# Opening of a fused attention and feed-forward kernel: constants moved between engines, statistics in tiles of their own, later queries in another PSUM bank

## The chip, the cores and the metric

The kernel runs on one core of one Trainium2 chip. The metric is the device time of one execution in microseconds (us), given as the median of several runs. PE is TensorE's matrix multiply, PEld its weight load, DVE is VectorE, ACT is ScalarE and POOL is GpSimd.

## The reference

One transformer block on 2048 rows of 512 features: layer norm, attention with 32 heads of 16, a residual, layer norm, a gated feed-forward part with 1792 hidden features, a residual. Inputs are bfloat16. The code is shortened.

```python
def _A_ref(x, wqkv, wo):                      # H = 32, Dh = 16
    qkv = (x @ wqkv).reshape(B, S, 3, H, Dh).transpose(2, 0, 3, 1, 4)
    q, k, v = qkv[0], qkv[1], qkv[2]
    scores = jnp.einsum("bhqd,bhkd->bhqk", q, k) * (Dh ** -0.5)
    o = jnp.einsum("bhqk,bhkd->bhqd", softmax(scores), v)
    return o.transpose(0, 2, 1, 3).reshape(B, S, D) @ wo
# ... _B_ref: (sigmoid(x @ w_gate) * (x @ w_up)) @ w_down
h  = x + _A_ref(_layernorm(x), wqkv, wo)
h2 = h + _B_ref(_layernorm(h), w_gate, w_up, w_down)
```

What matters here is how the kernel gets the softmax's sum: a constant column next to V makes that sum a column of the product with V. V stands in a tile `Vaug` of 16 blocks of rows by 32 heads by 17 columns, whose 17th column is a constant, 0.5.

## The kernel before

A static planner in Python orders the opening. It ends with the first scores, and the first exp (an ACTIVATE into `pt`) is the start of the steady state, in which PE and ACT are both almost always busy. The parts that the change touches are these. First the constants:

```python
Vaug = const.tile([P, NT, H, VW], BF16)          # P=128, NT=16, H=32, VW=17, DH=16
QT = [const.tile([P, QC], BF16, name=f"QT{g}") for g in range(NG)]
QTB = const.tile([P, 2, QC], BF16, name="QTb")
# ...
nc.vector.memset(eps_t[:], 1e-5)
nc.scalar.activation(out=A0[:], in_=eps_t[:], func=ACT.Sqrt)     # "warm": loads the Sqrt table
fill = prep.tile([P, QC], BF16, name="fill")
nc.gpsimd.memset(fill[:], 1.0)
nc.gpsimd.memset(eps4_t[:], 4e-5)
nc.gpsimd.memset(power[:], -0.5)
ramp = prep.tile([P, 2, 32], BF16, name="ramp")
for k in range(32):
    nc.gpsimd.memset(ramp[:, 0, k:k + 1], float(k))
nc.gpsimd.tensor_scalar(out=eps4_t[:], in0=eps4_t[:], scalar1=1.0, scalar2=None, op0=ALU.mult)
# ...
nc.vector.memset(Vaug[:, :, :, DH:VW], 0.5)      # 512 elements of 2 bytes, 34 bytes apart
nc.vector.memset(QTB[:], 0.0)
nc.vector.memset(ident_bf[:], 0.0)
nc.vector.transpose(out=ramp[:, 1, :], in_=ramp[:, 0, :])        # then the identity and the masks
```

Then the order of the opening. Each word is an engine's letter and a task: `s` statistics of a row tile, `q` Sqrt, `r` reciprocal, `a` apply, `t` transpose, `e` copy out of PSUM, `p0`/`p1` projection to keys/queries, `kt`/`qt` copies of keys and queries, `exps` the load of the exp table, `zero` the zeroing of a bank.

```python
START = "As1 Ds0 Ds2 Aq0 Dr0 Da0 Pt0 Aq2 Df1 Ds3 Aq1 Azero Ae0 Pp10 Dr2 Da2 Aq3 Aexps Dr1 Da1 Dr3 Da3 Pt2 De2 Pt1 Pp00 Pt3 Ae3 Pp12 De1 Pp01 Dkt0 Pp11 Dqt0 Pp13 Aqt1".split()
BANKS = {("t", 0): 5, ("t", 2): 7, ("t", 1): 6, ("t", 3): 1, 0: 2, 1: 3}

mvs = [small.tile([P, TQ, nc.vector.BN_AGGR_DIM], FP32, name="mv") for c in range(NQC)]
rstds = [small.tile([P, TQ], FP32, name="rstd") for c in range(NQC)]
def root(i):
    A.activation(out=rstds[0][:, i:i + 1], in_=mvs[0][:, i, 1:2], func=ACT.Sqrt, bias=eps_t[:, 0:1])
def proj0(which, i):
    ps = buf[which] if which in buf else buf.setdefault(which, bank0(which))
    for d in range(DC):
        E.matmul(ps[:, i * P:(i + 1) * P], lhsT=w0[:, which, d, :], rhs=xnv[0][:, i, d, :],
                 start=(d == 0), stop=(d == DC - 1))
def query0(half, a, act=False):
    cs = slice(0, QC) if half is None else slice(half * 2 * P, (half + 1) * 2 * P)
    # ... ACT or DVE: QT[a][:, cs] = buf[1][:, cs] * maskz[:, a]
# ... after the opening's words, the second query tile as a whole on DVE:
query0(None, 1)
```

Of the kernel before, what the change touches and what calls it, by code (L numbers as in the profile page):

```python
# [8 lines left out]
FP32 = mybir.dt.float32  # L9
# [5 lines left out]
ALU = mybir.AluOpType  # L15
ACT = mybir.ActivationFunctionType
# [5 lines left out]

START = "As1 Ds0 Ds2 Aq0 Dr0 Da0 Pt0 Aq2 Df1 Ds3 Aq1 Azero Ae0 Pp10 Dr2 Da2 Aq3 Aexps Dr1 Da1 Dr3 Da3 Pt2 De2 Pt1 Pp00 Pt3 Ae3 Pp12 De1 Pp01 Dkt0 Pp11 Dqt0 Pp13 Aqt1".split()

# [122 lines left out]
def kernel(  # L147
# [11 lines left out]
    nc = tc.nc  # L159
    P = 128  # L160
    S, D = A_x.shape[1], A_x.shape[2]
    H, DH = 32, 16
    F = B_w_gate.shape[1]
    NT = S // P
# [4 lines left out]
    QC = 512  # L169
    NQC = S // QC  # L170
    TQ = QC // P
# [12 lines left out]
    VW = DH + 1  # L184
# [21 lines left out]
    eps_t = const.tile([P, 1], FP32)  # L206
    eps4_t = const.tile([P, 1], FP32)
    mask = const.tile([P, 2], FP32)
    maskz = const.tile([P, 2], FP32)
# [3 lines left out]
    KT = [const.tile([P, S], BF16, name=f"KT{p}") for p in range(NP)]  # L213
    QT = [const.tile([P, QC], BF16, name=f"QT{g}") for g in range(NG)]
    QTB = const.tile([P, 2, QC], BF16, name="QTb")
    QTb = [QTB[:, a, :] for a in range(2)]
    Vaug = const.tile([P, NT, H, VW], BF16)
# [8 lines left out]
    xb = [prep.tile([P, TQ, D], BF16, name=f"xb{c}") for c in range(NQC)]  # L226
# [24 lines left out]
    nc.scalar.activation(out=A0[:], in_=eps_t[:], func=ACT.Sqrt)  # L251
    fill = prep.tile([P, QC], BF16, name="fill")
    nc.gpsimd.memset(fill[:], 1.0)
    nc.gpsimd.memset(eps4_t[:], 4e-5)
# [7 lines left out]
    acc = PS[:, 0, :]  # L262
    nc.vector.memset(Vaug[:, :, :, DH:VW], 0.5)
    nc.vector.memset(QTB[:], 0.0)
    nc.vector.memset(ident_bf[:], 0.0)
# [5 lines left out]
    def masks():  # L271
        nc.vector.tensor_reduce(out=mask[:], in_=ident_bf[:].rearrange("p (b a d) -> p a b d", a=2, d=DH),
                                axis=AX.XY, op=ALU.max)
        nc.vector.tensor_scalar(out=maskz[:], in0=mask[:], scalar1=ZS, scalar2=None, op0=ALU.mult)

    masks()

    def stats1(src, st):
# [55 lines left out]

    BANKS = {("t", 0): 5, ("t", 2): 7, ("t", 1): 6, ("t", 3): 1, 0: 2, 1: 3}

    def bank0(key):
        return PS[:, BANKS[key], :]

    mvs = [small.tile([P, TQ, nc.vector.BN_AGGR_DIM], FP32, name="mv") for c in range(NQC)]  # L340
    rstds = [small.tile([P, TQ], FP32, name="rstd") for c in range(NQC)]
    buf = {}
# [12 lines left out]
    V, A, E = nc.vector, nc.scalar, nc.tensor  # L355

    def stats_task(c, i):
        src, mv = xb[c][:, i, :], mvs[c][:, i, :]

        def on_act():  # L360
            junk = work.tile([P, D], BF16, name="junk")
            A.activation(out=junk[:], in_=src, func=ACT.Identity, scale=1.0 / D,
                         accum_out=mv[:, 0:1])
            A.activation(out=junk[:], in_=src, func=ACT.Square, scale=D ** -0.5,
                         accum_out=mv[:, 1:2])
            buf["fix", c, i] = True
        if c == 0:
            Task("s%d" % i, ["x%d" % i], A=(1480, on_act), D=(850, lambda: ln_stats(src, mv)))
            Task("f%d" % i, ["s%d" % i], D=(290, lambda: fix(c, i)))

    def fix(c, i):
        mv = mvs[c][:, i, :]
        if ("fix", c, i) in buf:
            t = small.tile([P, 1], FP32, name="fix")
            V.tensor_tensor(out=t[:], in0=mv[:, 0:1], in1=mv[:, 0:1], op=ALU.mult)
            V.tensor_tensor(out=mv[:, 1:2], in0=mv[:, 1:2], in1=t[:], op=ALU.subtract)

    def root(i):
        A.activation(out=rstds[0][:, i:i + 1], in_=mvs[0][:, i, 1:2], func=ACT.Sqrt, bias=eps_t[:, 0:1])

    def apply(c, i):
        xn = buf["xn", c, i] = prep.tile([P, D], BF16, name="xn0", bufs=4)
        V.tensor_scalar(out=xn[:], in0=xb[c][:, i, :], scalar1=mvs[c][:, i, 0:1],
                        scalar2=rstds[c][:, i:i + 1], op0=ALU.subtract, op1=ALU.mult)

# [6 lines left out]
    def proj0(which, i):  # L392
        ps = buf[which] if which in buf else buf.setdefault(which, bank0(which))
        for d in range(DC):
            E.matmul(ps[:, i * P:(i + 1) * P], lhsT=w0[:, which, d, :], rhs=xnv[0][:, i, d, :],
                     start=(d == 0), stop=(d == DC - 1))

    def keys0(half, act):
        cs = slice(half * 2 * P, (half + 1) * 2 * P)
        (A.copy if act else V.tensor_copy)(out=KT[0][:, cs], in_=buf[0][:, cs])  # L400

    def query0(half, a, act=False):
        cs = slice(0, QC) if half is None else slice(half * 2 * P, (half + 1) * 2 * P)
        if act:
            A.activation(out=QT[a][:, cs], in_=buf[1][:, cs], func=ACT.Identity, scale=maskz[:, a:a + 1])
        else:
            V.tensor_scalar(out=QT[a][:, cs], in0=buf[1][:, cs], scalar1=maskz[:, a:a + 1], scalar2=None,
                            op0=ALU.mult)
    fixed("w0", 6800.0)
    for i in range(TQ):  # L410
        fixed("x%d" % i, (3700.0, 3500.0, 4250.0, 4000.0)[i])
        stats_task(0, i)
        fixed_by = "f%d" if "As%d" % i in START else "s%d"
        Task("q%d" % i, [fixed_by % i], A=(310, lambda i=i: root(i)))
        Task("r%d" % i, ["q%d" % i], D=(110, lambda i=i: V.reciprocal(
            out=rstds[0][:, i:i + 1], in_=rstds[0][:, i:i + 1])))
        Task("a%d" % i, ["r%d" % i], D=(345, lambda i=i: apply(0, i)))
        Task("t%d" % i, ["a%d" % i], P=(300, lambda i=i: turn0(0, i)))
        Task("e%d" % i, ["t%d" % i], A=(550, lambda i=i: copy0(0, i, A.copy)),
             D=(430, lambda i=i: copy0(0, i, V.tensor_copy)))  # L420
        for w in (1, 0):
            Task("p%d%d" % (w, i), ["e%d" % i, "w0"], P=(280, lambda w=w, i=i: proj0(w, i)))
    for h in range(2):
        Task("qt%d" % h, ["p1%d" % (2 * h), "p1%d" % (2 * h + 1)],
             A=(460, lambda h=h: query0(h, 0, True)), D=(480, lambda h=h: query0(h, 0)))
# [3 lines left out]
        out=small.tile([P, 1], FP32, name="warm")[:], in_=eps_t[:], func=ACT.Exp)))  # L429
# [18 lines left out]
    for word in START:  # L448
        t, eng = tasks[word[1:]], word[0]
# [9 lines left out]
    keep_warm(go)  # L459

    for q in [QTB[:, 1, :]] + [q[:] for q in QT[2:]]:
        nc.sync.dma_start(out=q, in_=QTB[:, 0, :])
# [7 lines left out]
    LAT = 60.0  # L470
    TAIL = {"A": 150.0, "D": 85.0, "G": 100.0}
    T = {e: max(0.0, free[e] - go) for e in free}
# [135 lines left out]
    DRAIN = 170.0  # L608
# [636 lines left out]
    half = []  # L1245
# [153 lines left out]
    pe_time("dense", 560.0)  # L1399
    query0(None, 1)  # L1400
    T["D"] = max(T["D"] + 660.0, T["P"] + DRAIN + LAT) + 430.0
    keys0(1, False)
# [132 lines left out]
    for i in range(QB):  # L1535
        t = dvx.tile([P, 3, GQ, QC], I16, name="J", bufs=QB)[:].rearrange("p a b n -> p (a b n)")
# [24 lines left out]
    mv = small.tile([P, n, nc.vector.BN_AGGR_DIM], FP32, name="mvl")  # L1561
# [114 lines left out]
```

## Time and profile before

| | before |
|---|---|
| median (range), 3 runs | 732.33 us (732.21 to 732.76) |
| span of the profiled execution | 730.9 us |
| busy shares PE, ACT, DVE, POOL | 96, 96, 91, 58% |
| start of the first exp | 13.13 us |
| end of the opening on DVE (two copies) | 10.38 us |

The rows of a timeline are: start in us, length in us, engine, line of the kernel, operation, destination and source with their shapes, count, and in brackets how long the engine had stood idle and what ended it. The prediction shows the rows of DVE, and of ACT from 7.59 us on. The rows of ACT that stand ahead of them in the same timeline of the kernel before:

```profile
3.59 0.63 ACT L362 ACTIVATE junk<-xb 128x512 bf16<-128x512 bf16 x1 [0.45 <-DMA xb<-in_A_x_dram]
...
5.84 0.29 ACT L379 ACTIVATE rstd<-mv,eps_t 128x1 f32<-128x1 f32 x1 [0.77 <-DVE mv L282]
```

ACT makes the statistics of tile 1 as soon as its load has landed, and is then done so early that the first Sqrt stands 0.77 us for DVE's statistics of tile 0. ACT has slack here and DVE has none. That slack is what the change spends.

### The profile page before, as it was taken

What the parts mean: (1) busy time and instruction counts of PE and PEld (TensorE: products, weight loads), DVE (VectorE), ACT (ScalarE), POOL (GpSimd) and SP (SyncE); (2) the same over time, 40 slices, a digit from 0 to 9 for tenths busy, and PEclk for the clock granted to TensorE, in tenths of its full rate; (3) what the DMA queues carried; (4) which work ended last, traced back from release to release, by engine and by line L of the source; (5) the groups of instructions that cost most, each with busy time, mean ns of one, the idle gap of its engine ahead of it and who ended that gap; (6) DMA issues with size and microseconds to landing.
All of it is one profiled execution on the core that took longest, in us unless ns stands there. A gap on an engine that the chain in (4) does not pass through costs nothing.

```text
span 730.9 us, 26491 instructions
## 1 busy us (share of the span) xinstructions
PE 702.9 (96%) x11111; PEld 335.7 (46%) x11169; DVE 664.6 (91%) x1299; ACT 700.1 (96%) x786; POOL 426.4 (58%) x728
## 2 busy tenths in 40 slices
PE   8999999999999999999999999999999999999997
PEld 3222224444454445544545355535554455445564
DVE  7989989999999998999999999989999998999952
ACT  6999999999999999999999999999999999999962
POOL 2725657775566755646656766566664665666610
PEclk9999999999999999999999999999999999999999
DMA  8300006000223013321224023301322133013450
GB/s 272 74 10 11 11 8 178 2 2 3 74 70 102 15 32 103 89 45 46 67 61 109 9 82 88 74 17 44 106 66 60 39 103 103 10 24 88 120 157 19
DMA packets 85742, 47.39 MB, mean 65 GB/s; under 512 B 17521, under 2 KB 85617, under 8 KB 85617
## 3 DMA queue, kind: packets, MB, share of 16 engines
q1 hardware_dynamic: 85328, 45.37, 22.2%
q8 instruction: 89, 1.46, 0.8%
q14 instruction: 37, 0.29, 0.1%
q10 hardware_dynamic: 288, 0.26, 0.1%
HBM read 37.75 MB, written 2.10 MB: 55 GB/s over the span
## 4 chain that ended last, share of the span: by engine, by line
PE 64%; ACT 23%; DVE 7%; issue 4%; DMA 1%; POOL 1%; SPq 0%; DVEq 0%; ACTq 0%; POOLq 0%
PE PS L1061 22%; PE PS L1229 18%; ACT pt L1442 17%; PE PS L797 11%; PE PS L815 5%; DVE J L1253 3%; PE PS L319 3%; ACT xnT L1442 3%; PE PS L324 2%; ACT QTb L1442 1%; PE PS L740 1%; ACT th L827 1%; ACT xb L1442 1%; PE PS L1636 1%; POOL J L1274 1%
## 5 line engine op out<-in xcount | busy, mean ns | idle before, releaser
L1274 POOL INT64_ADD J<-J x658 | 407.9, 632 | 254.5 <-DVE J L1253 205.4
L1442 ACT ACTIVATE pt<-PS 128x1024 f16<-128x1024 f32 (+2 forms) x523 | 520.0, 1115 | 3.3 <-PE PS L1061 2.6
L1253 DVE TENSOR_SCALAR J<-PS 128x512 int16<-128x512 f32 x626 | 411.5, 678 | 18.5 <-PE PS L1061 13.1
L1061 PE MATMUL PS<-QT,KT 32*128 32x256 bf16 (+1 forms) x3712 | 264.0, 276 | 14.1 <-ACT pt L1442 5.8
L1229 PE MATMUL PS<-J,Vaug 128*17 128x256 f16 (+1 forms) x3195 | 226.1, 279 | 0.8 <-DVE J L1298 0.3
L1229 PE MATMUL PS<-pt,Vaug 128*17 128x256 f16 (+1 forms) x2042 | 198.4, 279 | 0.0
L1061 PEld LDWEIGHTS <-KT 32*128 32x128 bf16 x3840 | 89.7, 92 | 205.1 <-issue 201.3
L1229 PEld LDWEIGHTS <-Vaug 128*17 128x17 bf16 x5841 | 131.4, 90 | 78.5 <-issue 73.7
L797 PE MATMUL PS<-xnT,wgu 128*128 128x256 bf16 x784 | 112.9, 275 | 0.0
L1442 ACT ACTIVATE xnT<-PS 128x1024 f16<-128x1024 f32 (+1 forms) x85 | 92.3, 1116 | 0.5 <-PE PS L1061 0.2
L1298 DVE TENSOR_TENSOR J<-J 128x1024 f16<-128x1024 f16 (+1 forms) x110 | 78.4, 713 | 12.8 <-POOL J L1274 12.2
L797 PEld LDWEIGHTS <-wgu 128*128 128x128 bf16 x784 | 63.9, 98 | 38.6 <-issue 32.7
L815 PE MATMUL PS<-wd,hT 128*128 128x512 bf16 x167 | 50.2, 383 | 3.5 <-issue 3.5
L827 ACT ACTIVATE th<-PS 128x512 f32<-128x512 f32 (+1 forms) x63 | 38.8, 616 | 8.8 <-DVE hT L810 5.0
L1229 PE MATMUL PS<-xnT,Vaug 128*17 128x256 f16 x346 | 46.7, 274 | 0.0
L1442 ACT ACTIVATE QTb<-PS 128x1024 f16<-128x1024 f32 x40 | 44.0, 1100 | 0.0
L869 DVE SCALAR_TENSOR_TENSOR hT<-th,PS 128x512 bf16<-128x512 f32 x49 | 33.1, 676 | 0.8 <-PE PS L797 0.8
L1128 DVE STREAM_TRANSPOSE xs<-PS 128x256 f32<-128x256 f32 (+1 forms) x60 | 27.4, 458 | 1.7 <-PE PS L1229 1.4
L1442 ACT ACTIVATE xb<-PS 128x1024 f16<-128x1024 f32 (+1 forms) x25 | 26.0, 1086 | 0.7 <-issue 0.6
L1099 DVE TENSOR_TENSOR o<-xs,rsum 128x128 bf16<-128x128 f32 (+1 forms) x60 | 24.6, 410 | 2.1
L1229 PE MATMUL PS<-QTb,Vaug 128*17 128x256 f16 x160 | 25.7, 273 | 0.0
L1442 ACT ACTIVATE pe<-PS 128x1024 f16<-128x1024 f32 (+1 forms) x21 | 21.9, 1094 | 0.9 <-PE PS L1061 0.8
(125 smaller groups left out, 381.2 us busy)
## 6 DMA issues: line engine op xcount, KB each, us to landing
wgu<-in_B_w_gate_dram SPq DMA_DIRECT2D x49, 256.0 KB, 3.0
wgu<-in_B_w_up_dram SPq DMA_DIRECT2D x49, 256.0 KB, 3.5
out_dram<-ob SPq DMA_DIRECT2D x16, 128.0 KB, 1.8
QT<-qd SPq DMA_DIRECT2D x112, 16.0 KB, 1.8
wd<-in_B_w_down_dram SPq DMA_DIRECT2D x1, 1792.0 KB, 9.2
xr<-in_A_x_dram SPq DMA_DIRECT2D x14, 128.0 KB, 3.5
xb<-in_A_x_dram SPq DMA_DIRECT2D x6, 256.0 KB, 6.6
J<-in_B_w_gate_dram SPq DMA_DIRECT2D x4, 384.0 KB, 4.2
```

What stands on the lines that cost most here:

```text
L797: nc.tensor.matmul(ps[:, 0:PARTS[r][2]].rearrange("p (i q) -> p i q", q=P), lhsT=w[:, d, :], rhs=hn_of(r)[:, :, d, :], start=(d == 0), sto ...
L815: nc.tensor.matmul(ps, lhsT=hT[:, f, i * P:(i + 1) * P], rhs=wd[:, f, :], start=(f == 0), stop=(f == FC - 1))
L827: nc.scalar.activation(out=th[:, 0:ps.shape[-1]], in_=ps, func=ACT.Tanh, scale=0.5)
L869: nc.vector.scalar_tensor_tensor(out=hT[:, f:f + k, 0:w], in0=th[f][:].rearrange("p (k n) -> p k n", k=k), scalar=1.0, in1=ps2.rearrange(" ...
L1061: nc.tensor.matmul(pss[:, ui, i * CW[qc]:(i + 1) * CW[qc]], lhsT=KT[g // 2][32 * j:32 * j + 32, k * P:(k + 1) * P], rhs=q[32 * j:32 * j + ...
L1099: nc.vector.tensor_tensor(out=o2[:, 0:w // 32, DH * a:DH * a + DH], in0=xs[:, 0:w // 32, 0:DH], in1=rec.to_broadcast([P, w // 32, DH]), op ...
L1128: j = dve(650 - ns[0], lambda: nc.vector.transpose(out=xs[:, 0:w // 32, :].rearrange("p b r -> p (b r)"), in_=src), LAST, st["xs"], pr=-1)
L1229: nc.tensor.matmul(dst[32 * j:32 * j + VW, 0:w], lhsT=un.v[:, kt * SPAN[qc] + i, h, :], rhs=un.ap[:, i * w:(i + 1) * w], start=clears and ...
L1253: nc.vector.tensor_scalar(out=J[:, 0, k, :], in0=src, scalar1=ZOFF, scalar2=float(-min(CHORDS)), op0=ALU.add, op1=ALU.max)
L1274: nc.gpsimd.int64_add(words(s), words(0), CHORDS[s - 1] * (1 + 2 ** 16 + 2 ** 32 + 2 ** 48))
L1298: nc.vector.tensor_tensor(out=f1, in0=f1, in1=J[:, 0, 0:k, :].bitcast(FP16), op=ALU.add)
L1442: ex = nc.scalar.activation(out=pt, in_=pss[:, 0:wa, :], func=ACT.Exp, scale=AS)
```

## The change

The intent is to start the first exp sooner. Constants leave DVE's head: the column of `Vaug` goes to ACT, half of `QTB`'s zeroing goes behind the first scores and the other half goes away. The zeroing of the accumulator's bank goes behind the fourth copy. The later half of the queries gets bank 7, so that PE can write it while the first half is still read. Each row tile's statistics sit in a tile of their own (three floats in `QT4` to `QT7`, which are free then), so that no step waits for another tile's.

```diff
-START = "... Aq1 Azero Ae0 Pp10 ... Pt3 Ae3 Pp12 ..."
+START = "... Aq1 Ae0 Pp10 ... Pt3 Ae3 Azero Pp12 ..."
@@ constants
+    nc.scalar.activation(out=Vaug[:, :, :, DH:VW], in_=eps_t[:].to_broadcast([P, NT * H]).rearrange(
+        "p (t h o) -> p t h o", t=NT, o=1), func=ACT.Copy, scale=0.0, bias=0.5)
-    nc.vector.memset(Vaug[:, :, :, DH:VW], 0.5)
-    nc.vector.memset(QTB[:], 0.0)
@@ statistics
+    mv0 = [QT[4 + i][:, 0:6].bitcast(FP32) for i in range(TQ)]
-        A.activation(out=rstds[0][:, i:i + 1], in_=mvs[0][:, i, 1:2], func=ACT.Sqrt, bias=eps_t[:, 0:1])
+        A.activation(out=mv0[i][:, 2:3], in_=mv0[i][:, 1:2], func=ACT.Sqrt, bias=eps_t[:, 0:1])
     # ... the same in stats_task, fix, apply and the reciprocal
@@ banks
-    BANKS = {("t", 0): 5, ("t", 2): 7, ("t", 1): 6, ("t", 3): 1, 0: 2, 1: 3}
+    BANKS = {("t", 0): 5, ("t", 2): 7, ("t", 1): 6, ("t", 3): 1, (0, 0): 2, (0, 1): 2, (1, 0): 3, (1, 1): 7}
-        ps = buf[which] if which in buf else buf.setdefault(which, bank0(which))
+        ps = bank0((which, i // 2))
     # ... keys0 and query0 read bank0((which, half))
@@ after the first scores are planned
+    query0(0, 1)
+    query0(1, 1)
+    nc.vector.memset(QTB[:, 0, :], 0.0)
     for q in [QTB[:, 1, :]] + [q[:] for q in QT[2:]]:
         nc.sync.dma_start(out=q, in_=QTB[:, 0, :])
@@
-    query0(None, 1)
-    T["D"] = max(T["D"] + 660.0, T["P"] + DRAIN + LAT) + 430.0
+    T["D"] = max(T["D"] + 500.0, T["P"] + DRAIN + LAT) + 430.0
```

More of the change, by code (lines that the diff above doesn't have):

```diff
@@ L21 @@
 DependencyReason = mybir.DependencyReason
-START = "As1 Ds0 Ds2 Aq0 Dr0 Da0 Pt0 Aq2 Df1 Ds3 Aq1 Azero Ae0 Pp10 Dr2 Da2 Aq3 Aexps Dr1 Da1 Dr3 Da3 Pt2 De2 Pt1 Pp00 Pt3 Ae3 Pp12 De1 Pp01 Dkt0 Pp11 Dqt0 Pp13 Aqt1".split()
+START = "As1 Ds0 Ds2 Aq0 Dr0 Da0 Pt0 Aq2 Df1 Ds3 Aq1 Ae0 Pp10 Dr2 Da2 Aq3 Aexps Dr1 Da1 Dr3 Da3 Pt2 De2 Pt1 Pp00 Pt3 Ae3 Azero Pp12 De1 Pp01 Dkt0 Pp11 Dqt0 Pp13 Aqt1".split()
 PLAN = {64: 3, 128: 1, 144: 1, 172: 2, 192: 4, 273: 3, 274: 4, 289: 4, 300: 2, 351: 1, 495: 1, 496: 2, 508: 1, 524: 1, 545: 9, 546: 5, 560: 9, 562: 9, 700: 1, 703: 1, 732: 2, 748: 1, 769: 5, 831: 2, 881: 9, 882: 4, 894: 2, 1104: 1, 1120: 3, 1121: 9, 1137: 4, 1200: 2, 1217: 2, 1328: 5, 1409: 5, 1425: 2, 1473: 3, 1488: 2, 1503: 1, 1532: 1, 1534: 3, 1536: 9, 1552: 9, 1568: 3, 1584: 9, 1601: 4, 1630: 1, 1631: 2, 1660: 2, 1664: 3, 1692: 2, 1712: 1, 1905: 3, 1916: 2, 1936: 1, 2110: 2, 2124: 1, 2192: 2, 2288: 1, 2386: 1, 2396: 1, 2417: 3, 2478: 2, 2480: 9, 2482: 5, 2492: 1, 2512: 5, 2527: 2, 2560: 1, 2574: 1, 2577: 2, 2588: 2, 2658: 2, 2672: 9, 2689: 2, 2720: 9, 2722: 9, 2750: 1, 2752: 3, 2767: 1, 2769: 5, 2801: 9, 2816: 5, 2881: 4, 2924: 1, 2991: 1, 2994: 9, 3132: 1, 3185: 5, 3196: 2, 3217: 9, 3313: 3, 3393: 1, 3420: 1, 3456: 3, 3505: 3, 3564: 1, 3681: 9, 3692: 2, 3711: 2, 3760: 2, 3762: 9, 3778: 3, 3809: 3, 3823: 2, 3855: 2, 3873: 2, 3903: 2, 3905: 4, 3952: 3, 4032: 3, 4044: 2, 4066: 3, 4076: 2, 4097: 4, 4124: 1, 4144: 1, 4172: 1, 4176: 4, 4255: 2, 4320: 2, 4369: 9, 4386: 9, 4400: 1, 4416: 5, 4448: 3, 4496: 3, 4560: 9, 4622: 3, 4700: 1, 4796: 2, 4864: 4, 4928: 5, 4972: 2, 4977: 3, 4988: 1, 5006: 1, 5036: 2, 5042: 4, 5052: 2, 5056: 1, 5072: 2, 5088: 2, 5090: 4, 5106: 4, 5120: 3, 5122: 4, 5137: 5, 5153: 1, 5170: 4, 5184: 1, 5264: 2, 5298: 1, 5308: 1, 5314: 3, 5328: 3, 5404: 1, 5408: 4, 5423: 2, 5424: 4, 5425: 4, 5439: 2, 5441: 1, 5503: 1, 5521: 4, 5600: 3, 5649: 1, 5662: 2, 5698: 4, 5726: 3, 5728: 9, 5729: 4, 5777: 9, 5790: 1, 5792: 4, 5793: 3, 5794: 2, 5807: 2, 5824: 1, 5825: 4, 5840: 1, 5856: 3, 5889: 1, 5938: 4, 6178: 4, 6206: 3, 6256: 3, 6271: 1, 6302: 2, 6305: 9, 6318: 3, 6336: 2, 6337: 3, 6352: 4, 6354: 9, 6370: 9, 6417: 1, 6418: 1, 6448: 4, 6464: 1, 6510: 2, 6512: 2, 6513: 9, 6529: 2, 6562: 2, 6720: 4, 6862: 2, 6865: 9, 6881: 9, 6895: 2, 6944: 2, 6994: 3, 7214: 1, 7216: 3, 7282: 9, 7328: 4, 7362: 5, 7390: 3, 7393: 1, 7409: 9, 7438: 3, 7484: 1, 7566: 3, 7568: 4, 7632: 3, 7666: 9, 7676: 2, 7692: 2, 7698: 1, 7713: 1, 7728: 4, 7760: 4, 7777: 3, 7788: 1, 7824: 3, 7852: 2, 7856: 2, 7904: 1, 7916: 1, 7937: 3, 7952: 4, 7969: 1, 8000: 3, 8001: 9, 8097: 2, 8140: 1, 8176: 4, 8193: 3, 8225: 1, 8236: 1, 8270: 2, 8289: 9, 8303: 2, 8319: 2, 8337: 3, 8338: 1, 8348: 2, 8351: 2, 8352: 1, 8368: 2, 8369: 4, 8385: 3, 8386: 5, 8450: 3, 8476: 2, 8508: 2, 8512: 3, 8513: 3, 8530: 4, 8560: 4, 8577: 4, 8719: 2, 8721: 3, 8752: 1, 8802: 4, 8812: 1, 8860: 1, 9008: 4, 9072: 2, 9135: 2, 9182: 1, 9265: 9, 9296: 3, 9442: 2, 9489: 4, 9644: 1, 9680: 2, 9682: 4, 9745: 2, 9774: 2, 9777: 3, 9791: 1, 9793: 9, 9856: 5, 9872: 1, 10017: 9, 10028: 1, 10032: 5, 10079: 1, 10097: 3, 10127: 2, 10142: 3, 10144: 3, 10188: 1, 10256: 5, 10257: 9, 10268: 2, 10272: 9, 10351: 2, 10544: 1, 10636: 2, 10716: 1, 10719: 2, 10720: 3, 10736: 4, 10752: 1, 10764: 2, 10768: 9, 10770: 3, 11026: 5, 11057: 3, 11072: 3, 11087: 1, 11088: 2, 11120: 4, 11167: 2}
@@ L357, in stats_task @@
     def stats_task(c, i):
-        src, mv = xb[c][:, i, :], mvs[c][:, i, :]
+        src, mv = xb[c][:, i, :], mv0[i][:, 0:2]
         def on_act():
@@ L371, in fix @@
     def fix(c, i):
-        mv = mvs[c][:, i, :]
+        mv = mv0[i]
         if ("fix", c, i) in buf:
@@ L378, in root @@
     def root(i):
-        A.activation(out=rstds[0][:, i:i + 1], in_=mvs[0][:, i, 1:2], func=ACT.Sqrt, bias=eps_t[:, 0:1])
+        A.activation(out=mv0[i][:, 2:3], in_=mv0[i][:, 1:2], func=ACT.Sqrt, bias=eps_t[:, 0:1])
     def apply(c, i):
         xn = buf["xn", c, i] = prep.tile([P, D], BF16, name="xn0", bufs=4)
-        V.tensor_scalar(out=xn[:], in0=xb[c][:, i, :], scalar1=mvs[c][:, i, 0:1],
-                        scalar2=rstds[c][:, i:i + 1], op0=ALU.subtract, op1=ALU.mult)
+        V.tensor_scalar(out=xn[:], in0=xb[c][:, i, :], scalar1=mv0[i][:, 0:1],
+                        scalar2=mv0[i][:, 2:3], op0=ALU.subtract, op1=ALU.mult)
     def turn0(c, i):
@@ L399, in keys0 @@
         cs = slice(half * 2 * P, (half + 1) * 2 * P)
-        (A.copy if act else V.tensor_copy)(out=KT[0][:, cs], in_=buf[0][:, cs])
+        (A.copy if act else V.tensor_copy)(out=KT[0][:, cs], in_=bank0((0, half))[:, cs])
     def query0(half, a, act=False):
-        cs = slice(0, QC) if half is None else slice(half * 2 * P, (half + 1) * 2 * P)
+        cs = slice(half * 2 * P, (half + 1) * 2 * P)
+        src = bank0((1, half))[:, cs]
         if act:
-            A.activation(out=QT[a][:, cs], in_=buf[1][:, cs], func=ACT.Identity, scale=maskz[:, a:a + 1])
+            A.activation(out=QT[a][:, cs], in_=src, func=ACT.Identity, scale=maskz[:, a:a + 1])
         else:
-            V.tensor_scalar(out=QT[a][:, cs], in0=buf[1][:, cs], scalar1=maskz[:, a:a + 1], scalar2=None,
+            V.tensor_scalar(out=QT[a][:, cs], in0=src, scalar1=maskz[:, a:a + 1], scalar2=None,
                             op0=ALU.mult)
@@ L415 @@
         Task("r%d" % i, ["q%d" % i], D=(110, lambda i=i: V.reciprocal(
-            out=rstds[0][:, i:i + 1], in_=rstds[0][:, i:i + 1])))
+            out=mv0[i][:, 2:3], in_=mv0[i][:, 2:3])))
         Task("a%d" % i, ["r%d" % i], D=(345, lambda i=i: apply(0, i)))
```

## The prediction

> **What bounds the kernel now.** I read the page first, then busy time by stretch, then the timeline of the first 14 us, then its waits. The page says that two engines are full from the second slice to the last but one:
>
> ```profile
> PE 702.9 (96%) x11111; PEld 335.7 (46%) x11169; DVE 664.6 (91%) x1299; ACT 700.1 (96%) x786; POOL 426.4 (58%) x728
> PE   8999999999999999999999999999999999999997
> ACT  6999999999999999999999999999999999999962
> ```
>
> The change touches nothing but the opening, so the question is whether time won there survives. Busy time by stretch (after the length: PE, PEld, DVE, ACT, POOL):
>
> ```profile
> 13.13:34.40 21.27, 20.94 (x128) 6.42 (x130) 20.00 (x47) 20.91 (x24) 15.44 (x29) 1.00 0.49 131
> 60.00:700.00 640.00, 622.71 (x10584) 300.54 (x10634) 603.22 (x1156) 637.07 (x699) 400.97 (x646) 1.00 0.22 60
> ```
>
> From 13.13 us, where the first exp starts, ACT is busy 20.91 of 21.27 us and later 637.07 of 640. There is no slack in which a late start could be made up, nor one in which an early start must be lost, unless something tied to absolute time (a load) comes in between. So the whole price of the opening is the start of the first exp, 13.13 us. The timeline of the opening (start, length, engine, line, what) shows what sets it; rows of other engines are left out:
>
> ```profile
> 0.80 0.06 DVE L250 MEMSET eps_t<- 128x1 f32 x1 [0.80 <-PEq L1660]
> 2.58 0.48 DVE L263 MEMSET Vaug<- 128x512 bf16 x1 [1.72 <-issue]
> 3.10 0.48 DVE L264 MEMSET QTb<- 128x512 uint32 x1
> 3.54 0.11 DVE L265 MEMSET ident_bf<- 128x64 uint32 x1
> ...
> 4.90 0.69 DVE L279 BATCH_NORM_STATS2 st<-xb 128x6 f32<-128x512 bf16 x1
> ...
> 7.59 0.58 ACT L427 ACTIVATE PS<-eps_t 128x512 f32<-128x512 f32 x1
> ...
> 8.11 0.58 ACT L390 COPY xnT<-PS 128x512 bf16<-128x512 bf16 x1
> ...
> 9.63 0.75 DVE L390 COPY xnT<-PS 128x512 bf16<-128x512 bf16 x2
> ...
> 10.85 0.42 DVE L400 CAST KT<-PS 128x256 bf16<-128x256 f32 x1 [0.47 <-PE PS L395]
> 11.19 0.47 DVE L407 TENSOR_SCALAR QT<-PS,maskz 128x256 bf16<-128x256 f32 x1
> ...
> 11.73 0.40 PE L395 MATMUL PS<-xnT,w 128*128 128x128 bf16 x4 [0.69 <-DVE QT L407]
> ...
> 12.16 0.47 ACT L405 ACTIVATE QT<-PS,maskz 128x256 bf16<-128x256 f32 x1 [1.30 <-PE PS L395]
> ...
> 12.71 0.39 PE L1061 MATMUL PS<-QT,KT 32*128 32x512 bf16 x2
> ...
> 13.13 11.20 ACT L1442 ACTIVATE pt<-PS 128x1024 f16<-128x1024 f32 x12 [0.50 <-PE PS L1061]
> ```
>
> The reader is to see two chains. DVE runs without a hole from 2.58 to 10.38 us (the two copies end at 9.63 + 0.75), and the first thing in it that isn't needed yet is 0.96 us of memsets. Then, after 10.38, a ladder of five steps in which each waits for the one before: key projection, KT cast, first query half on DVE (11.19), the last query projection on PE (11.73, held by DVE's query read, as its bracket says), second query half on ACT (12.16), scores.
>
> **What the Trainium skill says.** "PSUM — Partial Sum Buffer", section "PSUM bank collisions raise a hardware error", asks for a guard by bank and quadrant, even of reads against reads. The trace agrees: the 11.73 matmul writes other columns of the bank that DVE reads, and still stood 0.69 us; the full second query tile on DVE (12.67) stood 1.00 us for ACT, which only reads the same bank. "VectorE: DVE Perf Modes", section "Zero memsets can be issued as uint32", says one cycle per element whatever the type: here 512 bf16 and 512 uint32 both take 0.48 us, 64 uint32 take 0.11, so half of QTb (256 words) should take about 0.27 us by interpolation, my estimate. "ScalarE: Activation LUTs", section "What ACT_TABLE_LOAD costs", gives 1283 ns for a table load, which the trace shows, and 186 ns + 0.833 ns per element for an ACTIVATE with immediates: 0.61 us at 512. The trace's zeroing ACTIVATE took 0.58, the next one starting 0.52 after it. I use these for the new Vaug fill.
>
> **The change part by part.** I compared the built order of both kernels: on every engine the instructions from the first exp on are the same in the same order, and PE's whole stream is the same but for three waits. The static planner therefore made no other decision.
>
> 1. Constants off VectorE. Vaug (2.58) and QTb (3.10) leave DVE's head; the identity's memset follows directly. From 3.54 to 2.58 is 0.96 us. It is possible only if its inputs are there: the ramp of 32 POOL memsets ends at 2.37; tile 0 lands at 0.73 + 3.0 = 3.73 and tile 2 about 4.6 (issue to landing, DMA view), before 3.94 and 4.76 when their statistics would start. So DVE's chain to 10.38 moves to 9.42.
> 2. The Vaug fill on ACT: about 0.6 us after the warm-up ACTIVATE of 2.93. ACT then waited 0.45 us for tile 1, to 3.59. Fill 3.05 to about 3.65: tile 1's statistics slip by under 0.1 us, ending near 5.1. The first Sqrt then starts near 5.1, not at 4.88, but its reciprocal is behind the second statistics on DVE anyway (5.55): no cost.
> 3. The zeroing of a bank (0.52 us of ACT at 7.59, between the last transposed tile and its copy) goes behind the fourth copy. The first copy moves by more than DVE's chain (8.11 to about 6.7), and the last Sqrt and the exp table load with it: table and warm-up end near 9.0 instead of 10.39. Before, the fourth copy was held by these to 10.29; now by its transposes, whose input ends at 8.75: 8.81 + 0.40 gives about 9.25 to 9.82. Zeroing then takes ACT to about 10.3.
> 4. Later queries in bank 7. The last query projection no longer waits for DVE's query half. It needs the fourth copy only: 9.86 to 10.26, not 11.73 to 12.13. ACT's query half: after zeroing and projection, 10.3 to 10.8. On DVE: KT cast 10.85 - 0.96 = 9.89, first query half 10.23 to 10.70. Both halves now end together. Scores follow at 10.85 (before: 0.08 after ACT's half), the first exp 0.42 later, at 11.27. The three warm-up matmuls ahead of the scores (0.22 us apiece) end about then: no cost.
> 5. Statistics in own tiles (columns of QT4 to QT7). In the built program each Sqrt already waited only for its own tile's last DVE step, before as after. Worth 0.
> 6. Added: QT1 in two halves (2 x 0.47 instead of 0.75 us) and 0.27 us of memset, on DVE between 10.7 and 11.8, where it waits for the second key half. That comes, as before, 0.97 us after the scores start: 11.8. QT1's second half ends near 11.5, before the second scores, about 11.7. The zero copies to QT2..QT7 start 2.8 us later, but the first real query copy into QT stands at 52.90: hidden.
>
> Sum: 13.13 - 11.27 = 1.86 us, of which 0.96 is item 1 and 0.90 is items 3 and 4 together (neither alone: without the move of the zeroing the copy stays late, without the other bank the ladder stays). I take off a tenth for steps that don't join so exactly: 1.7 us. 732.33 - 1.7 = 730.6 us.
>
> **Rivals.**
> - The Vaug fill is slow on ACT (512 single elements of 2 bytes, 34 bytes apart, and no trace line of ACT writing such a pattern). For it: the pattern is new. Against: DVE wrote the same pattern at the speed of dense words (0.48 both). With 1.2 us instead of 0.6, the first Sqrt ends near 6.0, DVE's chain slips 0.5: 731.1 us.
> - DVE's 1.72 us hole before 2.58 is "issue", unexplained. If it is instruction delivery and the next instruction is no sooner, item 1 holds as computed, since I start the identity at the same 2.58. If it grows, up to all of 0.96 is lost: 731.5 us. If it vanishes, the ramp (2.37) holds the start anyhow: 0.1 us better at most.
> - The gain is caught by a load. Value weights land at 3.77 + 6.4 = 10.2, first use 13.90 (12.1 after); second block of rows by about 9, used 14.03; POOL's own late start ends at 11.10, needed 15.81. All have over a microsecond to spare, so I give this a small chance: 732.
> - The first ladder step stays on DVE or ACT: if the second query half must wait for DVE's half after all, 0.4 us of item 4 is lost: 731.0. The built order speaks against it: ACT's wait there names an earlier copy.
>
> **Range and chances.** Best case, everything joins: 732.33 - 2.0 = 730.3, and 0.3 us for a luckier body: 730.0. Worst case at 8 in 10: half of item 1 or of item 4 lost, and 0.2 us of drift: 731.5. The spread of the runs before, 0.55 us, is inside this. All of it is 0.1 to 0.3% of the time: within 2% at 0.99, the two sides 0.005 each. An opening of 13 us, even wholly removed, is 1.8% of the time.
>
> **What would show it.** In the changed trace: identity memset near 2.6, first statistics near 3.9 (item 1); Vaug ACTIVATE under 0.7 us (item 2); first copy near 6.7 and exp table done near 9.0 (item 3); last query projection near 9.9 with no wait for the query read, first exp near 11.3 (item 4); ACT over 99% busy in the 640 us as before, with the same instructions everywhere. If the first exp stands near 11.3 and the time isn't 1.5 to 2 us lower, then my claim that the body moves rigidly is wrong. If the first exp is later than 11.9, one of items 1 to 4 is.

## The result and the profile after

| | before | after |
|---|---|---|
| median (range), 6 runs each | 732.49 us (732.21 to 733.21) | 731.43 us (730.98 to 732.22) |
| span of the profiled execution | 730.9 us | 729.3 us |
| first exp starts | 13.13 us | 12.68 us |

The ratio is 0.9986 with a 95% interval of 0.9973 to 0.9999. A ratio is the mean time of one kernel's runs over the mean of the other's of the same rounds, so it is not quite the ratio of the medians quoted. Executions over 1.5% slower than the fastest of the same kernel are left out of the means. The gain of 1.06 us between the medians is 0.14%. The predicted number (730.6) was too low by 0.8, inside its range by 0.07 us. The trace shows that the road to it was another one than predicted.

From the page of the kernel after, busy time of each engine and the row of slices of ACT; then its busy time by stretch:

```profile
PE 712.6 (98%) x11169; PEld 335.7 (46%) x11169; DVE 664.1 (91%) x1299; ACT 702.0 (96%) x787; POOL 426.4 (58%) x728
...
ACT  8999999999999999999999999999999999999962
```

```profile
60.00:700.00 640.00, 632.23 (x10637) 301.00 (x10637) 602.94 (x1155) 636.81 (x701) 401.00 (x646) 1.00 0.22 61
```

The body is what it was: ACT is busy 636.81 of 640 us, against 637.07. (PE's higher share is a matter of records: this trace holds all 11,169 matmuls, the one of before 58 fewer.) What is new is the first slice of ACT, 8 tenths instead of 6, and its busy time, 702.0 us instead of 700.1, with one instruction more. That instruction stands in the timeline of the opening:

```profile
0.85 0.11 DVE L265 MEMSET ident_bf<- 128x64 uint32 x1
...
3.04 2.36 ACT L253 ACTIVATE Vaug<-eps_t 128x512 bf16<-128x512 f32 x1
...
3.79 0.69 DVE L281 BATCH_NORM_STATS2 st<-xb 128x6 f32<-128x512 bf16 x1
...
4.93 0.89 ACT L364 ACTIVATE junk<-xb 128x512 bf16<-128x512 bf16 x1
...
6.57 0.46 ACT L381 ACTIVATE QT<-QT,eps_t 128x1 f32<-128x1 f32 x2
6.88 0.16 DVE L418 RECIPROCAL QT<-QT 128x1 f32<-128x1 f32 x1 [1.40 <-ACT QT L381]
...
7.99 0.58 ACT L392 COPY xnT<-PS 128x512 bf16<-128x512 bf16 x1
...
11.26 0.42 DVE L402 CAST KT<-PS 128x256 bf16<-128x256 f32 x1 [0.47 <-PE PS L397]
...
11.70 0.47 ACT L408 ACTIVATE QT<-PS,maskz 128x256 bf16<-128x256 f32 x1
12.24 0.10 PEld L1067 LDWEIGHTS <-KT 32*128 32x128 bf16 x2 [0.42 <-DVE QT L410]
12.24 0.39 PE L1067 MATMUL PS<-QT,KT 32*128 32x512 bf16 x2
```

Read from the top: DVE's first statistics now start at 3.79, 1.11 us earlier than before. The `Vaug` fill on ACT took 2.36 us. Behind it, the statistics of tile 1 start at 4.93 instead of 3.59, and the first Sqrt at 6.57 instead of 5.84. So DVE, which had gained 1.11 us, stood 1.40 us for that Sqrt, and the first reciprocal comes at 6.88. The fill has used up ACT's slack and then all that the head had won. Further down, the ladder is shorter as intended: the KT cast to the first exp takes 12.68 - 11.26 = 1.42 us, against 13.13 - 10.85 = 2.28.

The opening therefore gave 0.45 us. Where did the other 0.6 of the medians come from? These are rows of ACT's timeline at three places of the body, of the kernel before:

```profile
44.73 3.28 ACT L1442 ACTIVATE xb<-PS 128x1024 f16<-128x1024 f32 x3 [0.58 <-issue]
...
275.83 1.02 ACT L1442 ACTIVATE xnT<-PS 128x1024 f16<-128x1024 f32 x1
...
725.99 0.60 ACT L1639 ACTIVATE ob<-PS 128x512 bf16<-128x512 f32 x1 [2.42 <-PE PS L1636]
```

and of the kernel after:

```profile
43.89 3.28 ACT L1447 ACTIVATE xb<-PS 128x1024 f16<-128x1024 f32 x3 [0.19 <-issue]
...
274.45 1.02 ACT L1447 ACTIVATE xnT<-PS 128x1024 f16<-128x1024 f32 x1
...
724.61 0.60 ACT L1644 ACTIVATE ob<-PS 128x512 bf16<-128x512 f32 x1 [2.42 <-DMA out_dram<-ob]
```

The lead is 0.84 us after the row at 44 us (0.45 of the opening and 0.39 in that one wait, 0.58 against 0.19, where the engine waits for nothing that the profile shows). It is 1.38 us at 275 us and still 1.38 us at the end. Of the 0.54 us between 44 and 275 us, 0.3 lies in a wait of PE for a copy of queries by DMA (1.0 us before, 0.7 after, in the view of waits). The last rows are the end of the body, after which both kernels write out.

### The profile page after: what moved, and what is told of

Read it like the earlier page. It is cut to its first block, busy times and chain, and to the rows that moved or that the text cites. A ratio compares the mean times of both kernels' runs of the same rounds, so it can differ in the third digit from the quotient of the medians.

```text
span 729.3 us, 26553 instructions
## 1 busy us (share of the span) xinstructions
PE 712.6 (98%) x11169; PEld 335.7 (46%) x11169; DVE 664.1 (91%) x1299; ACT 702.0 (96%) x787; POOL 426.4 (58%) x728
## 4 chain that ended last, share of the span: by engine, by line
PE 69%; ACT 20%; DVE 7%; issue 2%; DMA 1%; POOL 1%; SPq 0%; ACTq 0%; DVEq 0%; POOLq 0%
PE PS L1067 23%; PE PS L1235 20%; ACT pt L1447 13%; PE PS L803 12%; PE PS L821 6%; DVE J L1259 3%; PE PS L321 3%; ACT xnT L1447 2%; PE PS L326 2%; PE PS L746 2%; ACT xb L1447 1%; ACT th L833 1%; ACT QTb L1447 1%; POOL J L1280 1%; DMA out_dram<-ob 1%
## 5 line engine op out<-in xcount | busy, mean ns | idle before, releaser
L821 PE MATMUL PS<-wd,hT 128*128 128x512 bf16 x196 | 56.7, 384 | 0.0
```

The lines of the kernel that those rows point to most:

```text
L821: nc.tensor.matmul(ps, lhsT=hT[:, f, i * P:(i + 1) * P], rhs=wd[:, f, :], start=(f == 0), stop=(f == FC - 1))
```

## The experiments

The theory that I tested: the strided fill costs over 2 us on ACT, it alone holds the opening at 12.68, and the rest of the change is worth what the prediction's chain says. The rivals: ACT is only late for another reason and the fill could stay there if it wrote dense; the separate bank, the zeroing or the own tiles are what doesn't work; and the gain in the body belongs to the change. There were twelve runs, in the order of the table: the first four on chip 1, the others on chip 0, so times are compared within the same rounds, and leads in the trace across them. The outputs of all twelve were right. In e3 and e4 a tile that is overwritten later (`KT[1]`) takes a dense fill of the same number of elements; the results stay right.

| run | median us (range), runs | ratio to before | first exp | wait near 44 us |
|---|---|---|---|---|
| after again | 731.52 (731.18 to 731.98), 5 | 0.9987 [0.9973, 1.0001] | 12.67 | 0.19 |
| e1, fill on POOL | 730.61 (730.09 to 732.06), 5 | 0.9979 [0.9965, 0.9992] | 11.31 | 0.50 |
| e2, fill on DVE, late | 732.03, 1 | | 11.28 | 0.62 |
| e3, dense fill on ACT | 730.70, 1 | | 11.61 | 0.19 |
| e10, fill split | 729.76 (729.45 to 730.49), 5 | 0.9957 [0.9944, 0.9971] | 11.16 | 0.30 |
| e11, before + 1 ACTIVATE | 731.55 (731.44 to 732.75), 5 | 0.9981 [0.9967, 0.9995] | 13.14 | 0.19 |
| e5, e1 with one query bank | 732.13, 1 | | 12.17 | 0.50 |
| e6, e1 with early zeroing | 731.50, 1 | | 11.35 | 0.56 |
| e4, before, dense fill on DVE | 730.87, 1 | | 12.17 | 0.50 |
| e9, before + bank only | 732.48, 1 | | 12.31 | 0.53 |
| e7, e1 with shared tiles | 729.69, 1 | | 11.40 | 0.50 |
| e12, e10 less 1 ACTIVATE | 729.97 (729.62 to 730.77), 6 | 0.9961 [0.9948, 0.9973] | 11.16 | 0.50 |

### The changed kernel again

No edit.

> The changed kernel again, unaltered, timed in the same rounds as the next run. Theory S (the opening alone changed: first exp 12.68 instead of 13.13 us, everything after it moves rigidly, and the rest of the 1.06 us between the medians is waits that differ from run to run): first exp at 12.68 within 0.1 us, time 0.3 to 0.8 us below before. Theory R (the changed opening really removes two later waits, at 44 and 274 us in the first trace): time 1.2 to 1.8 us below before, and this profile lacks the same two waits.

Measured: 731.52 us, 1.04 below before's 732.56 of the same rounds and so between what the two theories expected (the interval of the ratio just reaches 1); first exp 12.67, the wait near 44 us again 0.19. The lead in the body repeats, but the wait for the DMA copy of queries is 0.5 us here, not 0.7. What follows: opening and wait near 44 us belong to the kernel; the wait for that copy varies by run.

### e1: the fill on POOL

```diff
-    nc.scalar.activation(out=Vaug[:, :, :, DH:VW], in_=eps_t[:].to_broadcast(...), func=ACT.Copy, scale=0.0, bias=0.5)
+    nc.gpsimd.memset(Vaug[:, :, :, DH:VW], 0.5)      # after the ramp, before POOL's tensor_scalar
```

> The changed kernel with the Vaug fill moved from ACT to POOL, behind the 32 ramp memsets. Theory A (the 2.36 us fill on ACT delayed tile 1's statistics and the first Sqrt, and with it DVE by 1.40 us): the Sqrt starts near 4.9, DVE has no hole there, first exp near 11.1 to 11.3 (13.13 - 1.11 for the head of DVE - 0.90 for bank and zeroing), time 1.8 to 2.0 us below before and 1.3 to 1.5 below the changed kernel. Rival B (something else, such as the first copy or table load, is behind the late first exp): first exp stays above 12 us.

Two rows of the timeline of e1:

```profile
2.31 2.27 POOL L259 MEMSET Vaug<- 128x512 bf16 x1
...
11.31 2.85 ACT L1446 ACTIVATE pt<-PS 128x1024 f16<-128x1024 f32 x3 [0.50 <-PE PS L1066]
```

With the fill gone from ACT, the first Sqrt starts at 4.93, the reciprocal at 5.55, the first copy at 6.63 and the first exp at 11.31. This is the state that the prediction described (first copy near 6.7, first exp 11.27). Against the kernel after, every one of these steps is 1.3 to 1.6 us earlier, and 12.68 - 11.31 = 1.37 us reach the first exp. So it was the fill. It is no faster on POOL (2.27 us), but POOL has nothing else to do there.

The median gained 0.91 us over after (730.61 against 731.52 in the same rounds), not 1.37. Two things were lost again, and part of that came back later. The wait near 44 us is back at 0.50 (0.31 lost), and the stretch from the first exp to the row that stands at 34.40 in before grew from 21.27 to 32.88 - 11.31 = 21.57 us (0.30 lost). The latter goes with POOL: its first `tensor_scalar`, which ended at 11.81 in the kernel after, now ends at 14.99, 10.15 us after the fill, in a stretch that the profile calls issue, and the normalisation of the next rows waits for it. The later it runs, the more is lost: it starts at 14.73 here, at 15.62 in e3 and at 16.33 in e5, with the same fill on POOL, and the stretch there is 22.17 (33.78 - 11.61) and 22.42 us (34.59 - 12.17), so 0.90 and 1.15 are lost. Why it stands so long after the fill is open. The lead of e1 over after is 0.76 us at the row near 44 us (43.89 - 43.13) and 0.97 at ACT's last row (724.61 - 723.64).

### e2: the fill on DVE, behind the first scores

```diff
-    nc.scalar.activation(out=Vaug[:, :, :, DH:VW], ...)
     nc.vector.memset(QTB[:, 0, :], 0.0)
+    nc.vector.memset(Vaug[:, :, :, DH:VW], 0.5)
```

> The changed kernel with the Vaug fill back on DVE, behind the QTb memset after the query halves. If a DVE memset of this pattern costs the 0.48 us of its record: second key cast about 0.3 us late, first exp near 11.1 to 11.3 as with POOL, and DVE's statistics of block 1 start at most 0.4 us later than there. If it really costs about 2.2 us, of which the profile of before shows 0.48 as a record and 1.72 as a hole called issue: a hole of about 1.7 us before the fill's record, statistics of block 1 about 2 us later than with POOL.

```profile
13.31 0.48 DVE L465 MEMSET Vaug<- 128x512 bf16 x1 [1.70 <-issue]
```

The first exp starts at 11.28, as in e1. The row answers an open question of the kernel before: there, too, the memset of `Vaug` stood behind a hole (1.72 us, "issue"). The hole has moved with the memset, from 0.86 to 11.61 us. It is not the start of the program or of the engine, it belongs to this instruction, and its record of 0.48 us shows the tail only. The true cost on DVE is 1.70 + 0.48 = 2.18 us. It delays DVE's next statistics to 13.97, which is in the way of the next rows; the single run took 732.03 us.

### e3: a dense fill in the place of the strided one

```diff
-    nc.scalar.activation(out=Vaug[:, :, :, DH:VW], in_=..., func=ACT.Copy, scale=0.0, bias=0.5)
+    nc.scalar.activation(out=KT[1][:, 0:QC], in_=eps_t[:].to_broadcast([P, NT * H]), func=ACT.Copy, scale=0.0, bias=0.5)
+    # and Vaug on POOL as in e1
```

> The fill on POOL as in the run before, and on ACT in its old place a fill of the same 512 elements of 2 bytes, dense, into a tile that is overwritten later. If the 34-byte stride of the elements is what made ACT's fill slow: 0.55 to 0.65 us for it, and first exp within 0.1 us of the POOL version. If a 2-byte output to SBUF or the broadcast source is: above 1.5 us, and first exp near 12.7 again.

```profile
3.04 0.61 ACT L253 ACTIVATE KT<-eps_t 128x512 bf16<-128x512 f32 x1
```

The same operation on the same engine at the same time, with as many elements of the same type, took 0.61 us when they lie side by side and 2.36 us when they lie 34 bytes apart. (The packed trace records the output as one run of 512 elements in both. The source differs too: one value repeated over 16 x 32 there and over 512 here. The memsets of DVE and POOL, which have no source, are as slow at 34 bytes.) The 0.61 is what the prediction had put in for the strided one. The first exp came at 11.61, 0.30 later than in e1, where within 0.1 was expected. That is not the fill: PE's thirteen warm-up matmuls took 5.73 us in this execution (4.64 in e1), and the transposes behind them started at 6.83 instead of 6.19.

### e4: the kernel before, with a dense fill on DVE

```diff
-    nc.vector.memset(Vaug[:, :, :, DH:VW], 0.5)
+    nc.vector.memset(KT[1][:, 0:QC], 0.5)
+    nc.gpsimd.memset(Vaug[:, :, :, DH:VW], 0.5)      # on POOL as in e1
```

> The kernel before with DVE's strided Vaug memset replaced by a dense memset of as many elements into a tile that is overwritten later; the Vaug fill goes to POOL behind the ramp. If the stride is what cost DVE its 1.72 us hole: no hole, dense fill at 0.85 for 0.48, the second memset to about 1.85, transpose at 2.41 when the ramp is there, statistics of tile 0 at 3.8 instead of 4.90, first exp 12.0 to 12.2. If the hole is instruction delivery or start-up: it stands before the dense memset as well, 13.13.

```profile
0.94 0.48 DVE L264 MEMSET KT<- 128x512 bf16 x1
1.48 0.48 DVE L265 MEMSET QTb<- 128x512 uint32 x1
```

Without the stride there is no hole: the memset starts at 0.94 and the next follows at 1.48. The identity's memset, at 3.54 before, comes at 1.93, and the first exp at 12.17, 0.96 us earlier. This is the effect of item 1 of the prediction alone: here too the ramp holds DVE, to 2.41. DVE's statistics start 1.10 us earlier, of which 0.14 is lost again: the first of them took 0.82 us beside POOL's fill, not 0.69.

### e5: e1 with one bank for all the queries

```diff
-    BANKS = {..., (1, 0): 3, (1, 1): 7}
+    BANKS = {..., (1, 0): 3, (1, 1): 3}
```

> The POOL version with the later queries back in the bank of the first ones. Theory: the last query projection waits for DVE's first query half again (10.70), ACT's half follows, first exp about 12.1 instead of 11.31. If the bank is worth nothing once the zeroing is moved: 11.3.

```profile
10.76 0.40 PE L396 MATMUL PS<-xnT,w 128*128 128x128 bf16 x4 [0.69 <-DVE QT L409]
```

The wait of before is back (again 0.69 us, for DVE's read of the other half), and the first exp is 0.86 us later than in e1, at 12.17.

### e6: e1 with the zeroing ahead of the first copy

```diff
-START = "... Aq1 Ae0 Pp10 ... Ae3 Azero Pp12 ..."
+START = "... Aq1 Azero Ae0 Pp10 ... Ae3 Pp12 ..."
```

> The POOL version with the zeroing of the bank back ahead of the first copy. Theory: first copy and table load 0.5 us later, the fourth copy held by the table load to about 9.5, but ACT free of the zeroing afterwards: first exp 11.4 to 11.6, so 0.1 to 0.3 us later than 11.31. If the move of the zeroing is worth its whole 0.52 us: 11.8.

Measured: first copy at 7.15 instead of 6.63, fourth copy at 9.34 instead of 9.25, first exp at 11.35 instead of 11.31, so the loss is smaller than expected. The move of the zeroing is worth 0.04 us. It frees the first copy, which nothing on the path was waiting for.

### e9: the kernel before with the banks alone

```diff
-    BANKS = {..., 0: 2, 1: 3}
+    BANKS = {..., (0, 0): 2, (0, 1): 2, (1, 0): 3, (1, 1): 7}
     # ... proj0, keys0 and query0 by half, the second query tile in two halves
```

> The kernel before with the later queries in bank 7 alone (and with it the second query tile in two halves); constants and zeroing as before. Theory: the last query projection follows the fourth copy, about 10.95, ACT's query half 11.4 to 11.9, first exp 12.3 to 12.5, so 0.65 to 0.85 earlier. If, as the prediction had it, the bank needs the move of the zeroing as well: 13.1.

Measured: first exp at 12.31 instead of 13.13, 0.82 us from the banks alone. It is the same as in e5, from the other end. The single time, 732.48 us, lies among those of before; with a single run I can't say what became of the 0.82. Its trace shows a part: ACT is 1.26 us ahead at the row near 275 us, but PE then stands 0.58 us for DVE at 608.81, which it doesn't do in the profile of before, and ACT's last row is 0.50 ahead (725.49 against 725.99). The same wait stands in e5 and e11 and in none of the other eleven profiles; what brings it is open.

### e7: e1 with the statistics in shared tiles

```diff
-    mv0 = [QT[4 + i][:, 0:6].bitcast(FP32) for i in range(TQ)]
-    A.activation(out=mv0[i][:, 2:3], in_=mv0[i][:, 1:2], ...)
+    A.activation(out=rstds[0][:, i:i + 1], in_=mvs[0][:, i, 1:2], ...)   # and so on, as before
```

> The POOL version with the statistics of the four row tiles back in one shared tile each. Theory (each Sqrt waits for its own tile's last DVE step in either form): Sqrt starts within 0.05 us of the POOL version (4.93, 5.67, 6.43, 7.25) except where PE's clock start moves the copy, first exp 11.2 to 11.6. If own tiles matter: the second Sqrt waits for the first reciprocal, and the first exp is over 11.8.

Measured: the first three Sqrts start at 4.96, 5.67 and 6.43, in e1 at 4.93, 5.67 and 6.43. The fourth (7.67 against 7.25) stands behind the first copy, which PE's warm-up held: the transposes started at 6.77 instead of 6.19. First exp 11.40. Own tiles change no wait. The time of this single run, 729.69 us, was even below e1's five; I draw nothing from it.

### e10: the fill where nothing waits

Since the fill costs the same everywhere, I put it where the engine stands anyway. DVE is idle from 0.96 to 2.41 us, until the ramp is there, and 9 of the 16 blocks fit in. The other 7 go to POOL, but behind its first `tensor_scalar`, so that e1's delay doesn't arise. One more ACTIVATE of a single element is added, for the wait near 44 us.

```diff
-    nc.scalar.activation(out=Vaug[:, :, :, DH:VW], ...)
+    nc.scalar.activation(out=A0[:], in_=eps_t[:], func=ACT.Sqrt)      # the warm one a second time
     nc.vector.memset(ident_bf[:], 0.0)
+    nc.vector.memset(Vaug[:, 0:9, :, DH:VW], 0.5)
     nc.gpsimd.tensor_scalar(out=eps4_t[:], in0=eps4_t[:], ...)
+    nc.gpsimd.memset(Vaug[:, 9:NT, :, DH:VW], 0.5)
```

> A version meant to beat both: no Vaug fill on ACT; nine sixteenths of it on DVE in the hole in which DVE waits for POOL's ramp (0.96 to 2.41 us in the changed kernel), the rest on POOL behind its late first tensor operation; and one more 128x1 ACTIVATE in ACT's idle time before tile 1, to keep ACT's instruction count that of the changed kernel. Theory: at 4.3 ns per strided element the DVE part takes 1.24 us and fits the hole, statistics start at 3.8 as in the changed kernel, first exp 11.1 to 11.4, POOL ready before 13 us (14.73 in the POOL version), wait of ACT at 43 us 0.19 instead of 0.5: 729.6 to 730.3 us, 2.2 to 2.9 below before. If the fill on DVE hurts after all, first exp above 11.8.

```profile
1.89 0.30 DVE L266 MEMSET Vaug<- 128x288 bf16 x1 [0.93 <-issue]
...
11.11 1.05 POOL L261 MEMSET Vaug<- 128x224 bf16 x1
...
11.16 3.77 ACT L1448 ACTIVATE pt<-PS 128x1024 f16<-128x1024 f32 x4 [0.50 <-PE PS L1068]
```

DVE's part fits (the ramp's transpose still starts at 2.41), and POOL's `tensor_scalar` runs at 10.89, as early as in e2, which has no fill on POOL. The first exp starts at 11.16, 1.97 us earlier than before (and 0.15 earlier than in e1, where DVE's first statistics took 0.81 us beside POOL's fill and not 0.69), and the stretch behind it is 32.42 - 11.16 = 21.26 us again. The wait near 44 us was 0.30, not the 0.19 expected. The median is 729.76 us, a ratio of 0.9957; before's median in these rounds was 733.27, and against the 732.49 of the first rounds the gain is 2.7 us. This version beats both kernels: its slowest run (730.49) is faster than the fastest of before in the same rounds (732.20), and than the fastest of after (730.98, in other rounds, so that this second comparison is the weaker one).

### e11: the kernel before with one more ACTIVATE

```diff
     nc.scalar.activation(out=A0[:], in_=eps_t[:], func=ACT.Sqrt)
+    nc.scalar.activation(out=A0[:], in_=eps_t[:], func=ACT.Sqrt)
```

> The kernel before with nothing but one more 128x1 ACTIVATE on ACT, in the 0.45 us in which it waits for tile 1. Theory F (the wait called issue before an exp at 44.7 us, 0.58 us in before and 0.50 to 0.62 in the two runs with its number of ACT instructions, but 0.19 in the three runs with one more, goes with the place of instructions in ACT's stream): opening as before, first exp 13.13, that wait 0.19, time 0.3 to 0.8 us below before. Theory R (the wait differs by chance): 0.5 to 0.6 as in before, time within 0.3 us of before.

```profile
44.34 3.28 ACT L1443 ACTIVATE xb<-PS 128x1024 f16<-128x1024 f32 x3 [0.19 <-issue]
```

The opening is unchanged (first exp 13.14), and the wait near 44 us is 0.19 us instead of 0.58. In the table it goes with the number of ACT's instructions: with one more (after twice, e3, e10, e11) it is 0.19, 0.19, 0.19, 0.30 and 0.19; in the nine without, 0.50 to 0.62. So these 0.39 us are not of the change's ideas: an instruction that does nothing gets them too. It looks like the delivery of instructions to ACT, of which the count decides which one stands at a boundary; that is argued, no run shows it. The median, 731.55, is lower than 0.39 accounts for. Before's runs in those rounds fall in two groups, near 732.4 and near 733.3 us, and what parts them is open, so I take no more than the 0.39 from it. The profiled run of e11 was its slowest (732.75): in it the lead is still 0.35 us at 594 us, then comes the wait of 0.58 us for DVE that e9 has too (here at 609.63), and ACT's last row is 0.32 behind before's (726.31 against 725.99).

### e12: e10 without that ACTIVATE

> The split version without the extra ACTIVATE. Theory F (place in ACT's instruction stream): first exp 11.1 to 11.4 as with it, the wait of ACT at 42 to 43 us 0.5 to 0.6 instead of 0.30, time 0.2 to 0.4 us more. If that wait is chance: no difference in either.

```diff
-    nc.scalar.activation(out=A0[:], in_=eps_t[:], func=ACT.Sqrt)      # e10's second one
```

Measured: first exp 11.16 again, wait near 44 us 0.50 instead of 0.30, median 729.97 against 729.76. The trace shows 0.20 us; the medians agree with it, but the intervals of the two ratios overlap almost wholly, so in the time it is inconclusive.

## Why the prediction was right or wrong

The number was in the range, by luck. The main reason was wrong in size, and part of the distance was made up by something that the prediction did not have: without the 0.39 us near 44 us, the median would have been about 731.8 by my estimate (731.43 + 0.39), outside the range that ended at 731.5.

- **The bound and the price.** Right: the opening is the price, and what doesn't delay the first exp is free. The body did not move as rigidly as claimed, though. 0.45 us of lead in the opening became 1.38 at the end, through the wait near 44 us (0.39) and the stretch from there to 275 us (0.54, of which 0.3 is the DMA wait that varies by run). The remaining 0.24 comes at one exp, which starts at 265.81 before and at 264.73 after; what ended there is not traced, but in e11, with the opening of before, 0.22 appears at the same exp.
- **Item 1, constants off DVE.** Right: predicted 0.96 us. DVE's statistics came 1.11 earlier, since the hole went too and the ramp then held the start, as the second rival said (its "0.1 us better" was 0.15). Alone it gave 0.96 at the first exp (e4).
- **Item 2, the `Vaug` fill: the step that failed.** The prediction put it at "about 0.6 us ... no cost". It measured 2.36. The mechanism that it names (the first Sqrt moves back, then DVE's reciprocal) is the one that happened; the term was mis-sized by a factor of four. With 1.37 us of delay, which e1 measures, the prediction's own chain gives 11.27 + 1.37 = 12.64 us, and 12.68 was measured. The first rival named just this and was put aside with "DVE wrote the same pattern at the speed of dense words". That reading took a record at its word and left the 1.72 us ahead of it unexplained as another rival. The two were one thing: 1.72 + 0.48 = 2.20 us was the fill (e2, e4). The Trainium skill held a hint that the prediction did not look up. "SBUF — State Buffer", section "Door 1: The DMA port swizzle", says that SBUF has lines of 16 bytes and that each access which crosses to a new line pays. At 34 bytes every element is in another line. The measured 2.36 against 0.61 us agrees in direction; the page gives no size, and no run tried a third stride, so the line as the cause is argued, not shown. That the fill is slow because its elements don't lie side by side is shown by e3 and e4.
- **Items 3 and 4, zeroing and bank.** The sum of 0.90 is nearly right: both together gave 0.86 (from 12.17 in e4, which has neither, to 11.31 in e1). Of this the bank alone is 0.82 (e9), and the zeroing adds 0.04 (e6); without the bank it adds nothing (12.17 in e5 too). "Neither alone" is wrong: the bank alone does it. The prediction had the fourth copy late because of the exp table; in e6 that copy starts only 0.09 us later than in e1, although the zeroing stands ahead of the first. The trace of before held a sign of it: the transposes for that copy ended at 9.77 + 0.40 = 10.17, so the table load held it, to 10.29, for about 0.1 us at most.
- **Item 5, own tiles.** Right: worth 0 (e7).
- **Item 6, added work.** Right: in the kernel after, the second half of QT1 ends at 12.86, and the second scores start at 13.12, 0.88 us after the first; before it was 0.87.
- **Loads and the second query half.** Neither rival came true: no load appears in the chain, and ACT's query half starts at 11.70, right behind the zeroing.

Together: the prediction's 1.86 us in the opening exist (e1 has 13.13 - 11.31 = 1.82), the change as written paid 1.37 of them for the fill, and 0.39 came back in the body for an unrelated reason. From 732.49 that makes 732.49 - 0.45 - 0.39 = 731.65 us, where 731.43 was measured.

## What to carry to other kernels

Before moving a fill to another engine, read its cost as the record plus any unexplained idle time ahead of it on its own engine, and look at its stride before its element count; a record may show only the tail, as DVE's did here (those of ACT and POOL showed the whole). If the cost is the same everywhere, look for a place where an engine stands anyway, and split the work to fit it, as e10 does. And compare the lead of the new kernel at several times of the body, not only at the end: a lead that grows where nothing was changed isn't the change's until a run without the change has failed to show it.

## What the Trainium skill lacked or had wrong

- "VectorE: DVE Perf Modes", section "Zero memsets can be issued as uint32", gives one cycle per element whatever the type. The dense case agrees (512 elements in 0.48 us). For 2-byte elements 34 bytes apart it does not hold: 1.70 + 0.48 us for 512 and 0.93 + 0.30 for 288, both about 4.3 ns per element. The record itself shows only 0.48 and 0.30 us; the rest is a hole ahead of it.
- "ScalarE: Activation LUTs", section "What ACT_TABLE_LOAD costs", gives 186 ns + 0.833 ns per element. The dense output agrees (0.61 us for 512), the one with the 34-byte step took 2.36 us.
- "SBUF — State Buffer" says that a new 16-byte line costs, but not how much or on which engine ("GPSIMD Engine Reference", section "Performance pitfalls for Q7 kernels", has a figure for reads, none for writes). Here the step of 34 bytes took the writes to about 4.3 ns per element on DVE, and to 2.27 us for 512 on POOL, where a dense fill of 512 took 0.52.
- "TensorE: Matmul & The Clock Gate", section "What's actually happening", says that the activity window runs freely, so that the cold start differs from run to run, by 500 ns either way. That it differs agrees, but by more: counted from the first warm-up matmul, the steps of the matmuls fell to half (0.43 to 0.22 us for 512 columns) after 2.8 us in e10, and only after 5.8 in e3 (there during the transposes). This matters in an opening: the same thirteen warm-up matmuls took 4.28 to 5.73 us, and in e3 and e7 they moved the first transposes by 0.6 us.
- No page that I read gives the wait of ACT near 44 us (if it is the delivery of instructions, it belongs to "Runtime: NRT & Kernel Launch", section "Instruction fetch mechanics"), whose length (0.19 to 0.30 or 0.50 to 0.62 us) goes with one instruction more or less in ACT's stream (e11), or POOL's first `tensor_scalar`, which ran at 10.89 us without a fill ahead of it and at 14.73 with one of 2.27 us (e1).
